# A Fourier filter and mixture-of-experts kernel: first transfers on one queue, a matrix partly built by GpSimd, copies by two engines, stores issued by SP

## The chip, the cores and the metric

The kernel runs on one core of a Trainium2 chip. The metric is the device time of one execution in microseconds. An execution of the kernel before was profiled by the hardware; all rows below are from it.

## What is computed

The reference, cut to what matters:

```python
def _attn_ref(x, filt_r, filt_i):            # x: 8 x 2496 x 256
    X = np.fft.rfft(x, axis=1)
    Y = X * (filt_r + 1j * filt_i)[None]
    return np.fft.irfft(Y, n=x.shape[1], axis=1)

def _moe_ref(x, w_gate, w1, w2):             # 19968 tokens x 256, 8 experts
    logits = x @ w_gate
    order = np.argsort(-logits.flatten())
    for idx in order:                        # each expert takes up to N / E tokens
        ...
    for e in range(E):
        h = np.maximum(x[mask] @ w1[e], 0.0)
        out[mask] = h @ w2[e]
```

Everything is float32.

## The kernel before

The transform along the 2496 positions is split as 39 x 64. For each of the 8 batches there are these steps, all as matrix products on TensorE:

- **s1** (`Fft.s1`, line 201): 43 products of a 117-row slice of x with the constant `cS1`, in 11 tiles `t` of four products (the last has three). Each tile's result in PSUM is copied into `Y1` by four copies (line 207), `cp` and `ri` each 0 and 1. The PSUM pool has two such tiles (tag "a"). Each product stands in the trace as two records.
- **s2** (`Fft.s2`, line 214): ten units (g, dh), each four products of `Y1` with the second-step matrix `cW`; VectorE multiplies the result by the filter `F` (lines 220, 221), GpSimd combines the halves (lines 222, 223).
- **tr, trv** (lines 233, 242, 261): transposes back, and the logits' products with the gate.
- **inv1** (lines 269 to 283): ten inverse units q per batch, with the constants `cEh` and `cEl`; the result is copied to a tile `zt` (`ZB` = 4 buffers) and stored by two DMAs of 64 rows to `zd[b]` in DRAM.

Later `inv2` reads `zd` back and finishes the inverse; then the tokens are routed to experts, gathered, and run through two layers (lines 785 to 886). That later part is most of the span.

`Fft.run` puts steps into time slots with priorities (`at(slot, priority, ...)`), ten slots for a batch, and emits them in that order: s1 of batch b in slots 10b-10 to 10b, s2 from 10b, tr three and inv1 five slots behind. Batch b+1's s1 is so interleaved with batch b's s2. The tile framework's scheduler then orders each engine's queue; each engine runs its queue in order. Every DMA issued by SP or ACT takes the next of eight DMA semaphores, and a DMA that takes one again first waits for the transfer that had it.

The start, before: `consts` builds `cW`, 20 blocks of 128 x 128, each from `ab` and `cs` (one small load): ACT scales (line 154), VectorE multiplies and adds (line 155, two inputs in SBUF). `F` (2.6 MB) is loaded by two DMAs on ACT's queue (line 163); x of batch 0 by ten DMAs on SP's queue (line 189), x of batch 1 behind them; `consts3` stores zeros into the pads of the eight `zd` from ACT's queue (line 175) and loads `cEh` and `cEl` from GpSimd's queue once x of batch 1 is there (lines 178, 179). In batch 0 ACT makes all four copies of an even tile t, VectorE those of an odd one. The inverse units' stores are issued by ACT (line 283).

Of the kernel before, what the change touches and what calls it, by code (L numbers as in the profile page):

```python
# [7 lines left out]
F32, F32R = mybir.dt.float32, mybir.dt.float32r  # L8
# [101 lines left out]
def lay_filter(re, im):  # L110

    k, j = np.arange(K1)[:, None], np.arange(J)[None]
    fr = np.where(j < 32, k + 39 * j, 39 * (j - 31) - k)
    f = np.stack([np.asarray(re)[fr], np.asarray(im)[fr]])
    return np.ascontiguousarray(f.reshape(2, K1, J, 2, 128).transpose(4, 3, 1, 0, 2)).reshape(128, -1)


def lay_w1(w):
# [9 lines left out]
class Fft:  # L128
# [11 lines left out]
    def consts(s):  # L140
        nc, i = s.nc, s.i
        t = lambda n, sh: s.cp.tile(sh, F32, name=n)
        s.cS1 = t("cS1", [117, 120])
        s.F = s.wp.tile([128, 2, K1, 128], F32, name="F", tag="F", bufs=1)
        nc.sync.dma_start(s.cS1, i['cS1'])
        s.cW = s.wp.tile([128, K1, 128], F32, name="cW", tag="cW", bufs=1)
        q = s.wp.tile([128, 4, 128], F32, name="P", bufs=NP).rearrange("p k (m d) -> p (k m d)", m=1)
        nc.scalar.dma_start(q[:, :296], i['cW'])
        w = t("warm", [1, 2])
        nc.vector.memset(w, 0.0)  # L150
        nc.scalar.copy(w[:, 1:], w[:, :1])
        ab, cs = q[:, :256], q[:, 256:]
        for k in range(K1):
            nc.scalar.activation(s.cW[:, k], ab[:, :128], AF.Copy, scale=cs[:, k:k+1])
            nc.vector.scalar_tensor_tensor(s.cW[:, k], ab[:, 128:], cs[:, K1+k:K1+k+1], s.cW[:, k], op0=OP.mult, op1=OP.add)

    def consts2(s):
        nc, i = s.nc, s.i
        t = lambda n, sh, dt=F32: s.cp.tile(sh, dt, name=n)
        s.Vh, s.Vl = (s.cp.tile([128, K1, 64], F32R, name=n, tag=n, bufs=1) for n in ("Vh", "Vl"))  # L160
        s.id, s.gate = t("fid", [128, 128]), t("gate", [128, 2, 32])
        for dh in range(2):
            nc.scalar.dma_start(s.F[:, dh], i['filt'].rearrange("p (h k j) -> p h k j", h=2, k=K1)[:, dh])
        make_identity(nc, s.id)
        nc.gpsimd.memset(s.gate, 0.0)
        for h in range(2):
            nc.sync.dma_start(s.gate[:, h, :8], i['moe_w_gate'][128*h:128*h+128])

    def consts3(s):
        nc, i = s.nc, s.i  # L170

        q = s.wp.tile([128, 4, 128], F32, name="Q", bufs=1)
        nc.gpsimd.memset(q, 0.0)
        for zd in s.zd:
            nc.scalar.dma_start(zd[:, N2:], q[:40].rearrange("p k (n d) -> p (k n d)", n=1).rearrange("p (n d) -> p n d", n=2))
        s.cE = [s.cp.tile([128, K1, 128], F32R, name=n) for n in ("cEh", "cEl")]
        for c, nme in zip(s.cE, ("cEh", "cEl")):
            nc.gpsimd.tensor_copy(c[64:65, 0, :1], s.xr[1, 1][64:65, 0, 0, :1])
            nc.gpsimd.dma_start(c, i[nme].rearrange("p (k q) -> p k q", k=K1))

    def load_x(s, b, h, parts=1):

        w = 24 - 5*h
        xr = s.xr[b, h] = s.xp.tile([117, w, 2, N2], F32, name=f"xr{h}", bufs=2)
        v = s.i['x'][b].rearrange("p (q c n) -> p q c n", c=2, n=N2)
        for k in range(parts):
            q0, q1 = w*k//parts, w*(k+1)//parts
            for r in (slice(0, 112), slice(112, 117)):
                s.nc.sync.dma_start(xr[r, q0:q1], v[r, 24*h+q0:24*h+q1])

    def s1(s, b, t):

        nc = s.nc
        if t == 0:
            s.Y1[b] = s.wp.tile([128, K1, D], F32, name="Y1", tag="Y1", bufs=2)
        h = t // 6
        xv = s.xr[b, h].rearrange("p q c n -> p q (c n)")
        p = s.ps.tile([128, 4, 128], F32, name="p1", tag="a", bufs=2)
        q0, q1 = 4*t, min(4*t+4, 43)
        for q in range(q0, q1):  # L200
            s.lastmm = nc.tensor.matmul(p[:, q-q0, :120], xv[:, q-24*h], s.cS1, start=True, stop=True).ins  # L201
        for cp in range(2):
            for ri in range(2):
                src = p[64*cp:64*cp+64, :q1-q0, :120].rearrange("p q (b r k) -> p r k b q", b=3, r=2)[:, ri]
                a = s.Y1[b][64*ri:64*ri+64, :, 43*cp+q0:43*cp+q0+1]
                dst = bass.AP(tensor=a.tensor, offset=a.offset, ap=[list(a.ap[0]), [a.ap[1][0], K1], [85, 3], [1, q1-q0]])
                (nc.vector.tensor_copy if t in ((5,) if b else (1, 3, 5, 7, 9)) else nc.scalar.copy)(dst, src)  # L207

    def s2(s, b, g, dh):

        nc = s.nc
        p = s.ps.tile([128, 4, 128], F32, name="p2", tag="b", bufs=2)
        for k in range(4):
# [168 lines left out]
    def run(s, cp, wp, xp, ps, freed, prep, rest):  # L382
# [711 lines left out]
```

## Time and profile before

| | us |
|---|---|
| median of 3 runs (lowest, highest) | 1464.4 (1460.85, 1466.78) |
| the profiled execution's own time | 1464.14 |
| its span, first to last instruction | 1461.9 |
| TensorE busy in the span | 1387.9 |
| VectorE / ACT / GpSimd busy | 912.8 / 682.9 / 493.2 |
| first product of s1, batch 0 | 6.06 |
| first product of s2, batch 0 / 1 / 7 | 43.4 / 73.8 / 293.8 |

The own time is the span and 2.2 us around it. Engines in the rows are PE (TensorE matmul), PEld (its weight load), DVE (VectorE), ACT, POOL (GpSimd) and SP; a q behind the name is the engine's queue, which issues DMAs and waits. `out<-in` are tile names, `xN` a count. In a row of the timeline the bracket gives the idle time ahead of the piece and what ended it.

### The profile page before, as it was taken

To read this page: it belongs to the slowest core of one execution; us is meant where nothing else is said; L and a number is where in the kernel's file an instruction comes from. 1 tells how busy PE (TensorE), PEld (TensorE's weight loads), DVE (VectorE), ACT (ScalarE), POOL (GpSimd) and SP (SyncE) were. 2 spreads that over 40 slices of the span, in tenths; PEclk is the share of its full clock that TensorE was granted. 3 is DMA by queue.
4 is the path that set the end of the run, shared out by engine and by line. 5 is a ranking of instruction groups with operands and counts; after the bars stand their busy time and mean duration, and the time that the engine had idled before them with its cause. 6 is when DMAs were issued, how large, how long until landed. Compare 5 with 4: busy or idle time off the path is not lost.

```text
span 1461.9 us, 27147 instructions
## 1 busy us (share of the span) xinstructions
PE 1387.9 (95%) x10310; PEld 1214.2 (83%) x10310; DVE 912.8 (62%) x2589; ACT 682.9 (47%) x1676; POOL 493.2 (34%) x530
## 2 busy tenths in 40 slices
PE   4999999998896999999999999999999999999998
PEld 4998899985543898888889888898888899989988
DVE  3665666753666768767876977967876845333231
ACT  3666666644565425434533633633632635433232
POOL 0343333440102413522632443443325433333212
PEclk9999999998997999999999999999999999999999
DMA  9665564559996102212211211211211321111100
GB/s 266 182 165 141 145 176 99 119 157 280 297 352 219 57 26 91 64 36 75 69 43 58 73 50 48 86 48 41 98 34 54 132 70 46 39 48 49 42 23 27
DMA packets 56248, 150.60 MB, mean 103 GB/s; under 512 B 10824, under 2 KB 31432, under 8 KB 51921
## 3 DMA queue, kind: packets, MB, share of 16 engines
q0 software_dynamic: 17840, 60.34, 12.7%
q10 hardware_dynamic: 29407, 46.10, 10.5%
q1 hardware_dynamic: 8872, 42.44, 10.3%
q8 instruction: 81, 1.33, 0.4%
q14 instruction: 48, 0.39, 0.1%
HBM read 85.17 MB, written 63.70 MB: 102 GB/s over the span
## 4 chain that ended last, share of the span: by engine, by line
PE 68%; DVE 9%; issue 9%; ACT 6%; DMA 4%; ACTq 2%; POOL 2%; POOLq 0%; SPq 0%; DVEq 0%
PE py L867 23%; PE pz L824 22%; PE p L201 4%; PE pv L375 4%; PE p L214 4%; PE pa L269 2%; ACT Y L207 2%; PE rt L538 2%; PE ptr L802 2%; ACTq L283 2%; PE pa L233 2%; POOL out L878 1%; DMA xs<-xo 1%; ACT lg L698 1%; DMA wr<-w,widx 1%
## 5 line engine op out<-in xcount | busy, mean ns | idle before, releaser
L867 PE MATMUL py<-w1h,hl 128*128 128x256 f32 x2496 | 482.6, 286 | 1.1 <-DVE hl L835 1.0
L867 PEld LDWEIGHTS py<-w1h,hl 128*128 128x128 f32 x2496 | 401.1, 191 | 3.9 <-DVE hl L835 1.7
L867 PE MATMUL py<-w1l,hl 128*128 128x256 f32 (+1 forms) x1280 | 359.1, 282 | 0.0
L878 POOL DMA_INDIRECT out<-y,oid x160 | 171.9, 1074 | 495.6 <-ACT y L877 461.2
L830 ACT ACTIVATE hl<-pz 128x512 fp32r<-128x512 f32 (+1 forms) x320 | 187.2, 587 | 229.7 <-PE pz L824 206.1
L824 PE MATMUL pz<-xo,w0h 128*128 128x512 f32 (+1 forms) x640 | 263.9, 412 | 6.5 <-DVE hl L832 4.8
L832 DVE SCALAR_TENSOR_TENSOR hl<-pz,hl 128x512 fp32r<-128x512 f32 x256 | 174.9, 687 | 127.4 <-ACT hl L830 126.5
L824 PE MATMUL pz<-xo,w0l 128*128 128x512 f32 (+1 forms) x640 | 248.5, 388 | 0.0
L824 PE MATMUL pz<-z,w0h 128*128 128x512 f32 (+1 forms) x640 | 248.2, 388 | 0.3 <-DVE z L806 0.3
L867 PEld LDWEIGHTS py<-w1l,hl 128*128 128x128 f32 (+1 forms) x1280 | 241.1, 188 | 1.9
L788 POOL DMA_INDIRECT xg<-xs,xid x160 | 176.4, 1102 | 127.0 <-issue 44.5
L877 ACT COPY y<-py 128x256 f32<-128x256 f32 x152 | 56.4, 372 | 302.2 <-PE py L867 278.9
L207 ACT COPY Y<-p 64x240 f32<-64x240 f32 (+1 forms) x304 | 116.0, 382 | 60.7 <-PE pv L242 15.7
L824 PEld LDWEIGHTS pz<-xo,w0h 128*128 128x128 f32 x640 | 121.6, 190 | 24.8 <-DVE hl L832 6.2
L824 PEld LDWEIGHTS pz<-xo,w0l 128*128 128x128 f32 x640 | 120.6, 188 | 23.7
L824 PEld LDWEIGHTS pz<-z,w0h 128*128 128x128 f32 x640 | 121.7, 190 | 16.2 <-DVE z L806 0.9
L201 PE MATMUL p<-cS,xr 117*128 117x120 f32 x688 | 103.0, 299 | 29.3 <-ACT Y L207 20.1
L201 PEld LDWEIGHTS p<-cS,xr 117*128 117x128 f32 x688 | 93.7, 212 | 33.7 <-ACT Y L207 22.8
L222 POOL TENSOR_TENSOR P<-P 128x256 f32<-128x256 f32 x80 | 58.5, 732 | 172.4 <-DVE P L220 171.3
L530 DVE TENSOR_TENSOR Gm<-M,thr 117x1232 bf16<-117x1232 f32 (+2 forms) x80 | 104.4, 1315 | 0.2
L214 PE MATMUL p<-cW,Y 128*128 128x128 f32 x640 | 89.1, 278 | 0.7 <-ACT Y L207 0.7
L214 PEld LDWEIGHTS p<-cW,Y 128*128 128x128 f32 x640 | 80.2, 193 | 2.3 <-issue 1.0
(216 smaller groups left out, 2008.6 us busy)
## 6 DMA issues: line engine op xcount, KB each, us to landing
zd<-zt ACTq DMA_DIRECT2D x160, 128.0 KB
z<-zd SPq DMA_DIRECT2D x26, 600.0 KB
xs<-xo ACTq DMA_DIRECT2D x22, 600.0 KB
xr<-x SPq DMA_DIRECT2D x7, 1344.0 KB
xr<-x SPq DMA_DIRECT2D x7, 1064.0 KB
xs<-Y ACTq DMA_DIRECT2D x10, 600.0 KB
F<-filt ACTq DMA_DIRECT2D x2, 1280.0 KB
xg<-xs,xid POOLq DMA_INDIRECT x160, 2.8
```

The costliest lines, as they stand in the source:

```text
L201: s.lastmm = nc.tensor.matmul(p[:, q-q0, :120], xv[:, q-24*h], s.cS1, start=True, stop=True).ins
L207: (nc.vector.tensor_copy if t in ((5,) if b else (1, 3, 5, 7, 9)) else nc.scalar.copy)(dst, src)
L214: nc.tensor.matmul(p[:, k], s.Y1[b][:, 4*g+k, dh*128:dh*128+128], s.cW[:, 4*g+k], start=True, stop=True)
L222: nc.gpsimd.tensor_tensor(P[:, :, :64], P[:, :, :64], P[:, :, 64:], op=OP.subtract)
L375: nc.tensor.matmul(p[:120, :w], s.cD, z[:, g-g0:g-g0+w], start=True, stop=True)
L530: nc.vector.tensor_tensor(Gm[:, s0:s1, :m], s.M[:, s0:s1].unsqueeze(2).to_broadcast([117, s1 - s0, m]), thr[:117].unsqueeze(1).to_broadcas ...
L788: s.lastg = s.nc.gpsimd.indirect_dma_start(out=xg[:n], out_offset=None, in_=s.xs, in_offset=bass.IndirectOffsetOnAxis(ap=ids[0][:n, t:t+1] ...
L824: nc.tensor.matmul(p[:, :n], w[:, sl], x[:, k, :n], start=m == 0, stop=m == 5)
L830: s.lasta = nc.scalar.activation(h[:, :n], p[:, :n], AF.Relu).ins
L832: nc.vector.scalar_tensor_tensor(l[:, :n], p[:, :n], 0.0, h[:, :n].bitcast(F32), op0=OP.max, op1=OP.subtract)
L867: nc.tensor.matmul(p[:a.stop-a.start], hs[g][f][:, a], b[:, 256*f:256*f+256], start=m == 0, stop=m == 8 * len(terms) - 1, skip_group_check ...
L878: st = nc.gpsimd.indirect_dma_start(out=out_rows, out_offset=bass.IndirectOffsetOnAxis(ap=ids[1][:w, 4*g+t:4*g+t+1], axis=0), in_=y[:w], i ...
```

## The change

- `F`'s layout becomes five groups of g, each [2, 4, 128] per partition, and is loaded by five DMAs. All first loads go on SP's queue in order of need: x of batch 0 in five parts, then by turns one group of `F` and one part of x of batch 1. The gate's two small loads go to ACT's queue.
- The zero stores go to SP's queue, behind the first load of batch 2, from a tile of their own.
- ACT and VectorE build only blocks 0 to 7 of `cW`. GpSimd builds 8 to 19: for each g of 2, 3, 4 two products of 128 x 512 and one sum.
- `cEh` and `cEl` are loaded in two pieces each (blocks 0 to 7, then 8 to 19), from GpSimd's queue, when the first and the fifth unit of s2 are through.
- In batch 0 ACT makes the copies of `cp` 0 and VectorE those of `cp` 1, for every tile.
- Batches 0 to 5 have their inverse stores issued by SP; 6 and 7 still by ACT.

```diff
@@ consts
-        s.F = s.wp.tile([128, 2, K1, 128], F32, name="F", tag="F", bufs=1)
+        s.F = s.wp.tile([128, 5, 2, 4, 128], F32, name="F", tag="F", bufs=1)
...
-        for k in range(K1):
+        for k in range(8):
             nc.scalar.activation(s.cW[:, k], ab[:, :128], AF.Copy, scale=cs[:, k:k+1])
             nc.vector.scalar_tensor_tensor(s.cW[:, k], ab[:, 128:], cs[:, K1+k:K1+k+1], s.cW[:, k], op0=OP.mult, op1=OP.add)
+        for g in range(2, 5):
+            t = s.wp.tile([128, 2, D], F32, name="zt", bufs=ZB).rearrange("p k (m d) -> p (k m) d", m=2)
+            for m, o in enumerate((s.cW[:, 4*g:4*g+4], t)):
+                nc.gpsimd.tensor_tensor(o, ab[:, 128*m:128*m+128].unsqueeze(1).to_broadcast([128, 4, 128]),
+                                        cs[:, K1*m+4*g:K1*m+4*g+4].unsqueeze(2).to_broadcast([128, 4, 128]), op=OP.mult)
+            nc.gpsimd.tensor_tensor(s.cW[:, 4*g:4*g+4], s.cW[:, 4*g:4*g+4], t, op=OP.add)
@@ consts2
-        for dh in range(2):
-            nc.scalar.dma_start(s.F[:, dh], i['filt'].rearrange("p (h k j) -> p h k j", h=2, k=K1)[:, dh])
+        s.cE = [t(n, [128, K1, 128], F32R) for n in ("cEh", "cEl")]
+        for k, g in zip("FxFxFxFxFx", (0, 0, 1, 1, 2, 2, 3, 3, 4, 4)):
+            if k == "F":
+                nc.sync.dma_start(s.F[:, g], i['filt'][g].rearrange("p (h k j) -> p h k j", h=2, k=4))
+            else:
+                s.load_x(1, g // 3, *((g, 3) if g < 3 else (g - 3, 2)))
...
         for h in range(2):
-            nc.sync.dma_start(s.gate[:, h, :8], i['moe_w_gate'][128*h:128*h+128])
+            nc.scalar.dma_start(s.gate[:, h, :8], i['moe_w_gate'][128*h:128*h+128])
@@ consts3 becomes load_E and zeros
-            nc.scalar.dma_start(zd[:, N2:], q[:40].rearrange("p k (n d) -> p (k n d)", n=1).rearrange("p (n d) -> p n d", n=2))
...
-            nc.gpsimd.tensor_copy(c[64:65, 0, :1], s.xr[1, 1][64:65, 0, 0, :1])
-            nc.gpsimd.dma_start(c, i[nme].rearrange("p (k q) -> p k q", k=K1))
+    def load_E(s, g, k0, k1):
+        for c, nme in zip(s.cE, ("cEh", "cEl")):
+            s.nc.gpsimd.tensor_copy(c[:1, k0, :1], s.yt[0, g, 0][:1, 0, :1])
+            s.nc.gpsimd.dma_start(c[:, k0:k1], s.i[nme].rearrange("p (k q) -> p k q", k=K1)[:, k0:k1])
+    def zeros(s):
+        for zd in s.zd:
+            s.nc.sync.dma_start(zd[:, N2:], s.zero)
@@ s1
-                (nc.vector.tensor_copy if t in ((5,) if b else (1, 3, 5, 7, 9)) else nc.scalar.copy)(dst, src)
+                (nc.vector.tensor_copy if (t == 5 if b else cp) else nc.scalar.copy)(dst, src)
@@ inv1
-            nc.scalar.dma_start(s.zd[b].rearrange("a n c -> n a c")[:N2, 20*r+2*q:20*r+2*q+2], zt[64*r:64*r+64])
+            (nc.scalar if b >= B - 2 else nc.sync).dma_start(s.zd[b].rearrange("a n c -> n a c")[:N2, 20*r+2*q:20*r+2*q+2], zt[64*r:64*r+64])
@@ run
-        at(-12, 0, s.load_x, 0, 0, 3)
-        at(-12, 0, s.load_x, 0, 1, 2)
+        for k in range(5):
+            at(-12, 0, s.load_x, 0, k // 3, *((k, 3) if k < 3 else (k - 3, 2)))
         at(-12, 2, s.consts2)
-        for h in range(2):
-            at(-12, 3, s.load_x, 1, h)
-        at(-12, 4, s.consts3)
+        at(0.5, 1.5, s.load_E, 0, 0, 8)
+        at(4.5, 1.5, s.load_E, 2, 8, K1)
+        at(12, 9, s.zeros)
```

Lines behind the edits move: in the changed kernel s1's copy is line 217, s2's product 224, the inverse store 293.

ACT's queue at the start before, between its first loads and its first copies of s1:

```order
L163 DMA F<-filt 128x2560 x2
L175 DMA zd_60<-Q 40x512
L154 ACTIVATE cW<-P 128x128 x20
L175 DMA zd_61<-Q 40x512
L175 DMA zd_62<-Q 40x512
L175 DMA zd_63<-Q 40x512
L175 DMA zd_64<-Q 40x512
L175 DMA zd_65<-Q 40x512
L175 DMA zd_66<-Q 40x512
L175 DMA zd_67<-Q 40x512
L207 COPY Y_180<-p_181 64x20x3x4 x4
L207 COPY Y_180<-p_199 64x20x3x4 x4
```

and the same place with the change:

```order
L148 DMA P<-cW 128x296
L151 ACT_TABLE_LOAD
L151 COPY warm<-warm 1x1
L178 DMA gate<-moe_w_gate 128x8 x2
L154 ACTIVATE cW<-P 128x128 x8
L217 COPY Y_165<-p_166 64x20x3x4 x2
L217 COPY Y_165<-p_175 64x20x3x4 x2
```

The loads of `F` and all eight zero stores are gone from ACT's queue; ahead of its first copies stand eight scalings and two small loads.

GpSimd's queue with the change, from the identity matrix to the first pieces of `cEh` and `cEl` (P at line 159 is the tile of the small load; before, nothing of line 159 or 161 was there):

```order
masks.py:199 AFFINE_SELECT fid<-fid 128x128
L159 TENSOR_TENSOR cW<-P 128x512
L159 TENSOR_TENSOR zt<-P 128x512
L161 TENSOR_TENSOR cW<-cW,zt 128x512 x3
L232 TENSOR_TENSOR P<-P 128x4x64
L233 TENSOR_TENSOR P<-Q 128x4x64
L183 CAST cEh<-P 1x1
L183 CAST cEl<-P 1x1
L184 DMA cEh<-cEh 128x1024
L232 TENSOR_TENSOR P<-P 128x4x64
L184 DMA cEl<-cEl 128x1024
```

The two rows of line 159 stand there three times; nine instructions of 128 x 512 come ahead of GpSimd's part of s2. VectorE's queue with the change, from its start:

```order
L150 MEMSET warm 1x2
L155 SCALAR_TENSOR_TENSOR cW<-P,cW 128x128 x8
L217 COPY Y_165<-p_166 64x20x3x4 x2
L217 COPY Y_165<-p_175 64x20x3x4 x2
L217 COPY Y_165<-p_184 64x20x3x4 x2
```

All eight of line 155 stand ahead of VectorE's first copy of s1; before, nine stood there, and eleven more between its first three sets of copies.

SP's queue with the change, where batch 0's inverse stores begin (xr_461 and xr_705 are batch 3's x, xr_959 the first part of batch 4's):

```order
L199 DMA xr_461<-x 112x3072
L199 DMA xr_461<-x 5x3072
L293 DMA zd_60<-zt 64x2x256 x4
L199 DMA xr_705<-x 112x2432
L199 DMA xr_705<-x 5x2432
L293 DMA zd_60<-zt 64x2x256 x12
L199 DMA xr_959<-x 112x3072
L199 DMA xr_959<-x 5x3072
L293 DMA zd_60<-zt 64x2x256 x4
L293 DMA zd_61<-zt 64x2x256 x4
```

Before, SP's queue held only the loads of x there; the stores stood in ACT's queue between its copies.

## Rows read from the trace of the kernel before

**Rows 1.** The page's first line.

```profile
span 1461.9 us, 27147 instructions
```

**Rows 2.** By stretch: length, busy of PE, PEld, DVE, ACT, POOL; PEclk, DMA share, GB/s.

```profile
14.00:26.00 12.00, 0.01 (x1) 0.00 (x0) 0.62 (x3) 1.54 (x5) 0.00 (x0) 1.00 0.97 278
26.00:43.40 17.40, 16.42 (x71) 15.42 (x72) 6.50 (x16) 7.46 (x20) 1.63 (x4) 1.00 0.96 289
43.40:73.80 30.40, 30.40 (x280) 28.70 (x280) 20.09 (x35) 21.23 (x56) 14.57 (x20) 1.00 0.54 146
73.80:293.80 220.00, 210.86 (x2120) 198.33 (x2119) 148.52 (x273) 150.02 (x394) 89.55 (x135) 1.00 0.55 142
```

**Rows 3.** Timeline of PE, first 60 us: start, length, engine, line, operation, count.

```profile
6.06 3.74 PE L201 MATMUL p<-cS,xr 117*128 117x120 f32 x16 [6.06 <-DMA xr<-x]
...
26.02 14.99 PE L201 MATMUL p<-cS,xr 117*128 117x120 f32 x62 [12.01 <-ACT Y L207]
41.54 2.03 PE L201 MATMUL p<-cS,xr 117*128 117x120 f32 x8 [0.53 <-PE p L201]
43.37 1.93 PE L214 MATMUL p<-cW,Y 128*128 128x128 f32 x8
...
47.42 1.05 PE L201 MATMUL p<-cS,xr 117*128 117x120 f32 x8
...
57.89 0.37 PE L269 MATMUL pa<-yh,cEh 128*128 128x256 f32 x1
```

**Rows 4.** Timeline of ACT, first 45 us.

```profile
6.76 5.07 ACT L154 ACTIVATE cW<-P 128x128 f32<-128x128 f32 x17 [3.42 <-DMA P<-cW]
...
16.63 7.69 ACTq L175 DMA_DIRECT2D zd<-Q  x6
24.37 3.20 ACT L207 COPY Y<-p 64x240 f32<-64x240 f32 x8 [11.66 <-DMA zd<-Q]
```

**Rows 5.** The chain of waits in order of time, its first two pieces.

```profile
1.92 10.54 DMA F<-filt
12.78 9.81 DMA xr<-x
```

**Rows 6.** Weight loads of s1 (PEld, line 201) from 26 to 41 and 60 to 290.

```profile
L201 PEld LDWEIGHTS p<-cS,xr 117*128 117x128 f32 x62 | 13.5, 330 | 13.5 <-ACT Y L207 12.3 <-PE p L201 1.2
...
L201 PEld LDWEIGHTS p<-cS,xr 117*128 117x128 f32 x542 | 66.1, 192 | 10.8 <-ACT Y L207 10.5
```

**Rows 7.** Timeline of DVE, first 45 us.

```profile
7.20 2.69 DVE L155 SCALAR_TENSOR_TENSOR cW<-P,cW 128x128 f32<-128x128 f32 x9 [6.33 <-DMA xr<-x]
...
28.12 1.66 DVE L207 COPY Y<-p 64x240 f32<-64x240 f32 x4 [13.50 <-PE p L201]
```

**Rows 8.** Timeline of POOL and DVE, 369 to 379; DVE line 548: lowest, median, longest ns.

```profile
375.63 1.93 POOL L255 TENSOR_TENSOR yl<-Y,yh 128x512 fp32r<-128x512 f32 x1 [1.76 <-ACT yh L254]
377.50 1.30 POOL L255 TENSOR_TENSOR yl<-P,yh 128x512 fp32r<-128x512 f32 x1
...
377.72 1.16 DVE L548 TENSOR_TENSOR X<-D,row 112x56 f16<-112x56 f32 x1
...
L548 DVE TENSOR_TENSOR X<-D,row x77: 156/197/1162, 372.0 to 1130.8; 112x56 f16<-112x56 f32 x9, 112x49 f16<-112x49 f32 x9, 112x42 f16<-112x42 f32 x9, 112x35 f16<-112x35 f32 x9
```

**Rows 9.** What PE waited for, 73.8 to 293.8; ACT's timeline near 190.

```profile
PE p L201 <- ACT Y L207: 8.1, 13, 1.4
...
188.03 2.58 ACTq L283 DMA_DIRECT2D zd<-zt  x4
190.66 0.38 ACT L207 COPY Y<-p 64x240 f32<-64x240 f32 x1 [2.07 <-PE pv L242]
```

**Rows 10.** DMA issues: KB each, median us to landing; POOL's timeline at 34.

```profile
cEh<-cEh POOLq DMA_DIRECT2D x1, 1280.0 KB, 9.8
...
34.01 0.75 POOL L179 DMA_DIRECT2D cEh<-cEh  x1 [0.30 <-POOL cEl L178]
```

**Rows 11.** What SP's queue waited for, first 400 us: total, times, longest.

```profile
SPq L189 <- PE p L201: 65.1, 8, 14.0
```

More of the change, by code (lines that the diff above doesn't have):

```diff
@@ L114, in lay_filter @@
     f = np.stack([np.asarray(re)[fr], np.asarray(im)[fr]])
-    return np.ascontiguousarray(f.reshape(2, K1, J, 2, 128).transpose(4, 3, 1, 0, 2)).reshape(128, -1)
+    return np.ascontiguousarray(f.reshape(2, 5, 4, J, 2, 128).transpose(1, 5, 4, 2, 0, 3)).reshape(5, 128, -1)
 def lay_w1(w):
@@ L160, in consts2 @@
         s.Vh, s.Vl = (s.cp.tile([128, K1, 64], F32R, name=n, tag=n, bufs=1) for n in ("Vh", "Vl"))
-        s.id, s.gate = t("fid", [128, 128]), t("gate", [128, 2, 32])
-        for dh in range(2):
-            nc.scalar.dma_start(s.F[:, dh], i['filt'].rearrange("p (h k j) -> p h k j", h=2, k=K1)[:, dh])
+        s.id, s.gate, s.zero = t("fid", [128, 128]), t("gate", [128, 2, 32]), t("zero", [40, 2, D])
+        s.cE = [t(n, [128, K1, 128], F32R) for n in ("cEh", "cEl")]
[4 more added lines that the diff above has]
+                s.load_x(1, g // 3, *((g, 3) if g < 3 else (g - 3, 2)))
@@ L164, in consts2 @@
         make_identity(nc, s.id)
         nc.gpsimd.memset(s.gate, 0.0)
+        nc.gpsimd.memset(s.zero, 0.0)
         for h in range(2):
-            nc.sync.dma_start(s.gate[:, h, :8], i['moe_w_gate'][128*h:128*h+128])
[L169 to L173, printed above, removed]
-        for zd in s.zd:
-            nc.scalar.dma_start(zd[:, N2:], q[:40].rearrange("p k (n d) -> p (k n d)", n=1).rearrange("p (n d) -> p n d", n=2))
-        s.cE = [s.cp.tile([128, K1, 128], F32R, name=n) for n in ("cEh", "cEl")]
-        for c, nme in zip(s.cE, ("cEh", "cEl")):
-            nc.gpsimd.tensor_copy(c[64:65, 0, :1], s.xr[1, 1][64:65, 0, 0, :1])
-            nc.gpsimd.dma_start(c, i[nme].rearrange("p (k q) -> p k q", k=K1))
@@ L181, in load_x @@
-    def load_x(s, b, h, parts=1):
+            nc.scalar.dma_start(s.gate[:, h, :8], i['moe_w_gate'][128*h:128*h+128])
[4 more added lines that the diff above has]
+    def zeros(s):
+        for zd in s.zd:
+            s.nc.sync.dma_start(zd[:, N2:], s.zero)
+    def load_x(s, b, h, k=0, parts=1):
@@ L183, in load_x @@
         w = 24 - 5*h
-        xr = s.xr[b, h] = s.xp.tile([117, w, 2, N2], F32, name=f"xr{h}", bufs=2)
+        if k == 0:
+            s.xr[b, h] = s.xp.tile([117, w, 2, N2], F32, name=f"xr{h}", bufs=2)
+        xr = s.xr[b, h]
         v = s.i['x'][b].rearrange("p (q c n) -> p q c n", c=2, n=N2)
[L186 to L189, printed above, removed]
+        q0, q1 = 4*((w+3)//4*k//parts), min(4*((w+3)//4*(k+1)//parts), w)
@@ L191, in s1 @@
+        for r in (slice(0, 112), slice(112, 117)):
+            s.nc.sync.dma_start(xr[r, q0:q1], v[r, 24*h+q0:24*h+q1])
     def s1(s, b, t):
@@ L216, in s2 @@
         Q = s.wp.tile([128, 4, 128], F32, name="Q", bufs=1)
-        F = s.F[:, dh, 4*g:4*g+4]
+        F = s.F[:, g, dh]
         a = F[:, :, 64:65]
```

## The prediction

> **What bounds the kernel now.** First the sums by stretch [rows 2]. From 73.8 to 293.8 us TensorE is busy 210.86 of 220.00 us, so there TensorE is the limit and at most 220.00 - 210.86 = 9.1 us are to be had. From 14 to 26 us TensorE does nothing, at a DMA share of 0.97. The start is where the time lies. All that comes behind it hangs on TensorE's progress through the eight batches, so what s2 of batch 0 gains at its first product, at 43.37 us [rows 3], moves the rest forward as a whole, if nothing new holds it.
>
> Second, TensorE's timeline [rows 3]. Two tiles of s1 run at 6.06 us (16 records in 3.74 us); at 26.02 us TensorE starts again after 12.01 us in which it waited for ACT's copy of `Y`. Third, ACT's timeline at that place [rows 4]: its queue stands in the zero stores from 16.63 us for 7.69 us, and the first copy starts at 24.37 us, released by such a store. A store there waits for one of the eight DMA semaphores, so behind `F` and x. In the chain of waits [rows 5] this start is two transfers, `F` (10.54 us from 1.92) and x (9.81 us from 12.78). The two queues share the same traffic: x, which TensorE needs at once, came beside `F`, which nobody needs before 45 us.
>
> Fourth, the speed of TensorE. The clock column reads 1.00 throughout the first 74 us [rows 2], but a weight load of s1 takes 330 ns between 26 and 41 us and 192 ns later [rows 6], and eight records take 2.03 us at 41.54 and 1.05 us at 47.42 [rows 3]. So up to about 45 us TensorE was at the lower of its two levels (1.2 and 2.4 GHz), whatever the column says. Before it rose it had worked without a gap since 41.54 us, some 4 us; from 26 us on it had paused after every two tiles, the last time 0.53 us ahead of 41.54 (17.40 - 16.42 = 1.0 us in all [rows 2]).
>
> **The change part by part.** The sum is made against the profiled execution, 1464.1 us (span 1461.9 [rows 1] and 2.2 around it), 0.3 below the median of the runs.
>
> *Loads in order, zeros off ACT, copies by two engines.* These go together. The start of TensorE stays at about 6.1 us, since the first part of x already came ahead of `F`. The small load of `ab` and `cs` stays at 6.8 us, where ACT starts on it [rows 4]. With `F` behind it, x of batch 0 (2.6 MB, at the 278 GB/s of [rows 2] 9.3 us) is in by about 13 us. ACT now has eight scalings of 5.07 / 17 = 0.30 us, then copies. VectorE's eight multiply-adds take 2.69 / 9 x 8 = 2.4 us from 7.2 us on [rows 7], if nothing holds them, so its first copies would begin at 9.6 us. A tile's two copies take each engine 2 x 1.66 / 4 = 0.83 us [rows 7], so TensorE would go on at 9.6 + 0.83 + 0.1 = 10.6 us instead of 26.
>
> *`cW` by GpSimd: where I put the largest cost.* GpSimd's first product and VectorE's first multiply-add start together, when the small load lands. Both read two tiles in SBUF. The trace of before has this meeting once, far from here [rows 8]: a VectorE TENSOR_TENSOR of line 548, 197 ns in the median, took 1.16 us from 377.72, and ended at 378.88, just behind GpSimd's product of two SBUF tiles (377.50 to 378.80). So VectorE stood until GpSimd was nearly through. GpSimd's product of 128 x 512 took 1.30 us; the change has nine of that size, with some 0.08 us between, and eight multiply-adds on VectorE. If one multiply-add gets through per GpSimd instruction, the eighth ends with GpSimd's eighth, at 6.9 + 8 x 1.38 = 17.9 us and some tenths: 18.1. Bounds: no blocking (9.6 us), or one per instruction at the 1.93 us that GpSimd's longest one took while VectorE was in its way (6.9 + 8 x 2.01 = 23). I take one per instruction, 18.1 us, since [rows 8] is the same pair of engines with the same kinds of operands. It is the Trainium skill, "SBUF — State Buffer", section "Who interferes with whom", that makes this a rule: a VectorE instruction with two SBUF inputs and a GpSimd instruction that reads SBUF exclude each other, and the second to start waits for the whole of the first. The row shows it for a TENSOR_TENSOR; no row shows it for line 155's kind. By the rule the sum is the one below, by VectorE's own row [rows 7] without it the first rival's.
>
> *From there to s2.* TensorE resumes at 18.1 + 0.83 + 0.1 = 19.0 us, nine tiles left. At the lower level a tile takes 3.74 / 2 = 1.87 us [rows 3], more than the copies need; so TensorE works without a gap, and after 4 us, as from 41.54 us, I take it to rise. By 23 us 2.1 tiles are done. At the higher level a tile is 0.9 us of products; with copies (0.83) and the hand-overs (about 0.4) over two buffers it is (0.9 + 0.83 + 0.4) / 2 = 1.07 us: 6.9 x 1.07 = 7.4 us, so s1 ends at 30.4, and with the last copies and hand-overs (1.2 us) s2 begins at 31.6. Gain 43.4 - 31.6 = **11.8 us**. Had the level stayed low, nine tiles take 16.8 instead of 11.4 us: gain 6.4.
>
> *The lower level's tail.* The 2 us after 43.4 ran at half speed and won't: **1.0 us**.
>
> *Inverse stores to SP.* ACT's queue spends 2.58 us on four of them at 188.03, and the copy behind waits 2.07 us, marked as if for TensorE [rows 9]; the one large wait of TensorE in the eight batches is for ACT's copies, 8.1 us in 13 waits. Batches 0 to 5 are freed of 120 issues, at 0.65 us 77 us of ACT's queue. What TensorE can gain is between nothing and 9.1 us; VectorE's side of the same pipeline stays. I take two thirds, **6 us**. Against it stands the Trainium skill, "DMA: Bandwidth & Descriptors", section "Issuing engines are not separate DMA queues": choosing the issuing engine saves only its issue time, usually small beside the transfer. By that this part is about nothing and the time 6 us longer; the row at 190.66 speaks against it.
>
> *`cEh`, `cEl` in pieces.* GpSimd's queue now issues four loads inside s2; one took it 0.75 us [rows 10], with the casts about 2 us per pair. VectorE's `Q` has one buffer, so a late GpSimd can hold VectorE and then TensorE: 0 to 3 us, I take **1 us** lost, as GpSimd is busy only 14.57 of 30.40 us there. The first inverse needs the pieces 57.89 - 43.37 = 14.5 us behind s2's begin; a whole `cEh` landed in 9.8 us, and the first two pieces are 1 MB together, issued some 4 us behind s2's begin: about level, covered because `F` and x of batch 1 (5.2 MB, 19 us) are through by 32 us. If that cover went, it is 0 to 3 us.
>
> *The rest costs nothing.* GpSimd's nine instructions end at 6.9 + 9 x 1.38 = 19.3 us, with VectorE's share at 22, before s2 begins. The zero stores (0.6 MB) go behind batch 2's first load; only `inv2` reads them, near the end of the eight batches, and SP's queue had room. The gate's two small loads stand on ACT while it waits for the small load anyway.
>
> Sum: -11.8 - 1.0 - 6 + 1 = -17.8, so 1464.1 - 17.8 = 1446.3, **1446 us**.
>
> **The rivals.**
> *Less blocking than one per instruction.* If two multiply-adds slip through per GpSimd instruction, VectorE is free at about 13.6 us, 4.4 us earlier: 1442. If none is held, it is 9.6 us: 8.5 us earlier, 1437.7. For it: a multiply-add has 128 elements in a row and takes 0.35 us, about the pause between two GpSimd instructions; against it: [rows 8].
> *ACT's relief gives nothing.* TensorE's waits move to VectorE's copies or GpSimd: 1446 + 6 = 1452. For it: DVE is busy 148.52 of 220 us, as much as ACT's 150.02 [rows 2].
> *The level stays low, or GpSimd's products are longer.* The first costs 16.8 - 11.4 = 5.4 us, the second (1.93 us each) 23 - 18.1 = 4.9 us: 1451.
> *Slower: stores stuck behind x on SP.* SP's queue waited 65.1 us in 8 waits for TensorE to release x's buffers, at most 14.0 us [rows 11]; now 12 and 4 and 4 stores by turns stand behind such loads. An inverse unit comes every 220 / 60 = 3.7 us and `zt` has four buffers, so a store may be three units late, 11 us, before a copy waits for its buffer, then ACT or VectorE, then TensorE. At 14.0 us it costs 3 us for each of ten loads: 1446 + 30 = 1476. Against it: the order puts the s1 tile that releases x ahead of the inverse unit whose store stands behind that load, so the wait is over when the store is due.
>
> **How the numbers follow.** About 0.5% (7.3 us) is what a measurement of this kernel can tell from no change. The forecast has 0.45, its own range 1443 to 1450; less blocking 0.32; no relief 0.08; low level or longer products 0.08; stores stuck 0.04; small losses adding up to no change 0.03. Range 1435 to 1453: from 1437.7 less the 3 us of relief that I left out, to 1452 and one more. Faster: 0.45 + 0.32 + 0.08 + 0.08 = 0.93; same 0.03; slower 0.04.
>
> **What would show it.** In the changed kernel's timeline: VectorE's multiply-adds of 128 x 128 spread over 6.9 to 18 us, with GpSimd's products beside them; TensorE's second pair of tiles at about 19 us, s2's first product at 31.6; ACT's first copies straight behind its scalings; weight loads of s1 at 190 ns before s2 begins; the wait of s1 for ACT's copies far below 8.1 us between batch 1 and batch 7. Wrong: multiply-adds back to back in 2.4 us (then s2 near 23 us), s2's first product later than 37 us, TensorE waiting for `cEh`, or copies to `zt` that wait for a store.

## The result and the profile after

The changed kernel takes 1449.5 us (median of 5 runs, 1446.5 to 1452.6), the kernel before 1464.0 (5 runs): a ratio of 0.9897, with a 95% interval of 0.9881 to 0.9913. The forecast was 1446, from 1435 to 1453. The total is right; its split is not, as the rows show. The profiled execution took 1449.9 us.

By stretch, the changed kernel (columns as in [rows 2]):

```profile
0.00:36.00 36.00, 22.92 (x98) 21.44 (x99) 17.56 (x31) 12.61 (x34) 11.31 (x17) 1.00 0.99 240
36.00:66.00 30.00, 29.30 (x279) 27.13 (x277) 19.58 (x34) 22.67 (x59) 17.28 (x28) 1.00 1.04 266
66.00:104.00 38.00, 35.14 (x343) 33.57 (x344) 24.37 (x44) 24.30 (x63) 13.63 (x19) 0.96 0.59 149
104.00:290.00 186.00, 186.00 (x1916) 176.99 (x1916) 136.03 (x249) 133.88 (x342) 82.54 (x126) 1.00 0.57 144
```

and two of these stretches in the kernel before:

```profile
0.00:36.00 36.00, 15.47 (x66) 14.46 (x67) 10.75 (x34) 13.57 (x38) 2.89 (x12) 1.00 0.93 267
...
104.00:290.00 186.00, 176.86 (x1770) 166.01 (x1770) 124.16 (x228) 127.29 (x335) 74.15 (x113) 1.00 0.54 137
```

From 104 to 290 us TensorE now never stops: 1916 matmul records in the time in which it did 1770. Up to 36 us it does 98 where it did 66, but the transfers are slower, 240 GB/s against 267, at a DMA share of 0.99.

The start, in the timelines of DVE, POOL, ACT and PE of the changed kernel (they answer to [rows 7, 8, 4, 3]):

```profile
6.38 8.57 DVE L155 SCALAR_TENSOR_TENSOR cW<-P,cW 128x128 f32<-128x128 f32 x8 [5.52 <-ACT cW L154]
...
18.91 0.84 DVE L217 COPY Y<-p 64x240 f32<-64x240 f32 x2 [2.25 <-ACT Y L217]
```

```profile
6.00 1.03 POOL L159 TENSOR_TENSOR cW<-P 128x512 f32<-128x512 f32 x1 [4.14 <-DMA P<-cW]
7.00 1.08 POOL L159 TENSOR_TENSOR zt<-P 128x512 f32<-128x512 f32 x1
...
12.23 3.84 POOL L161 TENSOR_TENSOR cW<-cW,zt 128x512 f32<-128x512 f32 x3
```

```profile
18.12 0.76 ACT L217 COPY Y<-p 64x240 f32<-64x240 f32 x2 [7.81 <-PE p L211]
```

```profile
16.05 3.74 PE L211 MATMUL p<-cS,xr 117*128 117x120 f32 x16 [6.53 <-DMA xr<-x]
...
33.39 2.03 PE L211 MATMUL p<-cS,xr 117*128 117x120 f32 x8 [0.15 <-PE p L211]
35.22 1.46 PE L224 MATMUL p<-cW,Y 128*128 128x128 f32 x8
...
68.86 0.39 PE L279 MATMUL pa<-yh,cEl 128*128 128x256 f32 x1 [3.48 <-DMA cEl<-cEl]
...
70.86 1.92 PE L224 MATMUL p<-cW,Y 128*128 128x128 f32 x8
...
75.87 1.06 PE L224 MATMUL p<-cW,Y 128*128 128x128 f32 x8
```

Eight multiply-adds take 8.57 us beside GpSimd's first eight instructions: six products, one every 1.04 us, and two of the three sums, one every 1.27 us. They end at 14.95 us, the eighth GpSimd instruction at 14.80. At 16.05 us TensorE resumes, behind VectorE's first copies (from 14.96 us); the row names x, but `e2_pool_late`, below, resumes at the same tile at 10.94 us. VectorE's copies of a tile (18.91) begin when ScalarE's of the same tile (18.12, 0.76 us) are through. s2 begins at 35.22 us, 8.2 earlier than at [rows 3]. At 68.86 us TensorE has waited 3.48 us for the second piece of `cEl`, and behind that wait it is at its lower level: eight records take 1.92 us at 70.86 and 1.06 us at 75.87. In the chain of waits the piece is one long step:

```profile
52.34 16.48 DMA cEl<-cEl
```

To compare kernels whose order differs a little, I read from each trace when TensorE begins the matmul record with n others ahead of it: n = 94 is about s2's first, 700 lies near the end of batch 1, 2600 some 10 us behind the begin of batch 7's s2, 3290 where the routing's positions begin. The experiments ran on three chips, where the kernel before took 1490 us (`e1` to `e4`), 1496 us (`e5` to `e8`) and 1464 us (`e9` to `e12`), so times are compared as ratios to the kernel before on the same chip. Among the experiments only the second chip has a ratio of the changed kernel itself (`e5_after_again`). Times in the first four expectations are in the first result's us.

| kernel | n = 94 | 700 | 2600 | 3290 | ratio to before (95%) |
|---|---|---|---|---|---|
| before, first profile | 43.4 | 105.7 | 303.3 | 432.0 | |
| before, `e12_before_again` | 40.2 | 101.0 | 300.1 | 429.7 | |
| changed, first profile | 35.2 | 102.0 | 286.3 | 417.5 | 0.9897 (0.9881 to 0.9913) |
| changed, `e5_after_again` | 33.0 | 100.7 | 285.0 | 416.3 | 0.9855 (0.9831 to 0.9878) |
| `e1_act_stores` | 35.9 | 105.4 | 297.1 | 425.8 | 0.9951 (0.9930 to 0.9973) |
| `e7_before_sp` | 39.2 | 101.5 | 287.1 | 415.7 | 0.9917 (0.9885 to 0.9949) |
| `e2_pool_late` | 26.3 | 97.7 | 282.0 | 413.7 | 0.9839 (0.9815 to 0.9864) |
| `e4_nodep` | 27.9 | 97.6 | 281.9 | 413.6 | 0.9873 (0.9848 to 0.9897) |
| `e3_e_early` | 34.8 | 96.9 | 284.2 | 418.2 | 0.9885 (0.9857 to 0.9913) |
| `e6_all` | 22.3 | 99.8 | 284.0 | 413.2 | 0.9869 (0.9846 to 0.9893) |
| `e8_all_zero` | 21.4 | 92.5 | 278.2 | 411.9 | 0.9862 (0.9840 to 0.9885) |
| `e9_no_gpsimd` | 32.9 | 106.9 | 292.5 | 426.6 | 0.9924 (0.9894 to 0.9954) |
| `e11_f_act` | 36.0 | 97.6 | 283.2 | 411.9 | 0.9931 (0.9907 to 0.9954) |
| `e10_extra` | 34.4 | 101.2 | 285.5 | 421.0 | 0.9927 (0.9901 to 0.9953) |

With the two profiles of each kernel averaged, the change gains 7.7 us at n = 94, 2.0 at 700, 16.0 at 2600 and 14.0 at 3290. So of the start 5.7 us are lost again up to the end of batch 1 (the wait for `cEl` and the lower level behind it are there); 14 us come from 700 to 2600; 2 us go back behind.

### The profile page after: what moved, and what is told of

Its sections match the earlier page's. It is cut to its first block, busy times and chain, and to the rows that moved or that the text cites. A ratio compares the mean times of both kernels' runs of the same rounds, so it can differ in the third digit from the quotient of the medians.

```text
span 1448.1 us, 27257 instructions
## 1 busy us (share of the span) xinstructions
PE 1386.1 (96%) x10310; PEld 1214.4 (84%) x10310; DVE 918.3 (63%) x2579; ACT 683.4 (47%) x1662; POOL 503.9 (35%) x543
## 4 chain that ended last, share of the span: by engine, by line
PE 72%; DVE 9%; issue 8%; DMA 5%; ACT 3%; POOL 2%; ACTq 1%; POOLq 0%; DVEq 0%; SPq 0%
PE py L877 23%; PE pz L834 22%; PE p L211 5%; PE p L224 5%; PE pa L279 4%; PE pv L385 3%; PE pa L243 2%; PE rt L548 2%; PE ptr L812 2%; POOL out L888 1%; PE pv L252 1%; DMA xs<-xo 1%; DMA xr<-x 1%; DMA cEl<-cEl 1%; ACT lg L708 1%
## 5 line engine op out<-in xcount | busy, mean ns | idle before, releaser
L211 PEld LDWEIGHTS p<-cS,xr 117*128 117x128 f32 x688 | 93.6, 212 | 14.6 <-issue 14.6
L540 DVE TENSOR_TENSOR Gm<-M,thr 117x1232 bf16<-117x1232 f32 (+2 forms) x80 | 105.4, 1328 | 0.2
L224 PE MATMUL p<-cW,Y 128*128 128x128 f32 x640 | 92.4, 279 | 0.0
```

Of the source, the lines that this page charges most:

```text
L540: nc.vector.tensor_tensor(Gm[:, s0:s1, :m], s.M[:, s0:s1].unsqueeze(2).to_broadcast([117, s1 - s0, m]), thr[:117].unsqueeze(1).to_broadcas ...
```

## The experiments

**Theory:** ScalarE's relief brings the middle stretch, and the start is held by three things, the blocked multiply-adds, copies that go one after the other, and late transfers. **Rival:** the better start brings it all, and the stores' place is worth nothing.

**The stores' place, from both sides.** In `e1_act_stores` the changed kernel's stores go back to ScalarE; in `e7_before_sp` the kernel before gets them on SP, and nothing else.

```diff
-            (nc.scalar if b >= B - 2 else nc.sync).dma_start(s.zd[b] ...
+            nc.scalar.dma_start(s.zd[b] ...
```

> The changed kernel with the inverse stores issued by ScalarE again, all else kept. Theory (the stores' issues on ScalarE were what held TensorE up in batches 2 to 6): the stretch from the first second-step matmul of batch 2 to that of batch 7, 171.7 us in the changed kernel and 186.2 us before it, comes back to 184 to 187 us, TensorE waits for ScalarE's copies there again, and the kernel takes 1455 to 1464 us, of which the start's gain stays (first second-step matmul at about 35 us). Rival (the shorter stretch comes from the start's better order of transfers and the stores are worth nothing): the stretch stays at 171 to 174 us and the kernel takes 1449 to 1452 us.

> The kernel before with one part of the change alone: the inverse stores of batches 0 to 5 issued by SP, all else as before. Theory (the stores' issues on ScalarE held TensorE up in batches 2 to 6, and this part needs none of the others): the stretch from the first second-step matmul of batch 2 to that of batch 7 falls from 186.2 us to 171 to 174 us, the first second-step matmul stays at about 43 us, and the ratio to the kernel before is 0.990 to 0.994. Rival (SP then holds the stores behind x, or the relief needs the better start): the stretch stays at 180 us or more and the ratio is 0.996 to 1.002.

What TensorE waited for from 104 to 290 us, in `e1_act_stores`:

```profile
PE p L211 <- ACT Y L217: 5.7, 10, 1.2
```

in `e12_before_again`:

```profile
PE p L201 <- ACT Y L207: 8.2, 14, 1.9
```

and by stretch, in `e7_before_sp`:

```profile
104.00:290.00 186.00, 184.22 (x1900) 174.88 (x1900) 133.41 (x246) 134.07 (x344) 80.95 (x122) 1.00 0.58 147
```

From n = 700 to 2600 the two profiles of before take 197.6 and 199.1 us, `e7_before_sp` 185.6, the changed kernel 184.3 both times, `e1_act_stores` 191.7. So the stores' place alone brings 12 to 13.5 us of the 14 and needs none of the other parts; the rival falls. By the expectation's measure, s2 of batch 2 to s2 of batch 7, `e7_before_sp` takes 173.5 us, as expected. Undone, the stores' place costs 7.4 us from 700 to 2600, not 13 (182.7 us by the expectation's measure, a little under its 184 to 187), and 3 to 5 us more ahead of n = 700, which `e1_act_stores` reaches at 105.4 us, no earlier than before (105.7 and 101.0). At n = 2600 the part is worth 14.6 us alone and 11.4 us undone; all other parts together bring 1.5 us there with the stores on SP and 4.7 us with them on ScalarE. How the waits share out between them I can't assign. In the times `e1_act_stores` is 0.5% faster than before, `e7_before_sp` 0.8%; of the latter's six runs three took 1477 us and three 1485 to 1490, so its interval is wide. Still, on the same chip the changed kernel is faster than it (0.9855, and the intervals do not meet): in the times the stores' place alone is 14 of 21 us, though at the positions the two are level (415.7 and 416.3). What makes the rest of the difference stays open.

**The multiply-adds.** Before each GpSimd product one element of its output is written from column 7, which VectorE makes last, so that the products begin behind the multiply-adds:

```diff
             for m, o in enumerate((s.cW[:, 4*g:4*g+4], t)):
+                nc.gpsimd.tensor_copy(o[:1, 0, :1], s.cW[:1, 7, :1])
```

> The changed kernel with GpSimd's products made to start after VectorE's eighth multiply-add (each product's output is first written by a one-element copy out of matrix column 7). Theory (each of VectorE's multiply-adds was held for one GpSimd product): the eight multiply-adds take 0.2 to 0.4 us each and end at about 9 us instead of 14.95, TensorE resumes stage 1 of batch 0 at about 10 us instead of 16.05, the first second-step matmul comes at 29 to 31 us instead of 35.2, and the kernel takes 1443 to 1446 us. Rival (the parts of x or GpSimd's later products bound the start anyway): the multiply-adds end early but TensorE waits for x or for the matrix, the first second-step matmul comes at 33 us or later, and the kernel takes 1448 to 1451 us.

DVE's timeline in `e2_pool_late`,

```profile
7.02 2.40 DVE L155 SCALAR_TENSOR_TENSOR cW<-P,cW 128x128 f32<-128x128 f32 x8 [6.16 <-ACT cW L154]
```

and PE's:

```profile
10.94 3.74 PE L212 MATMUL p<-cS,xr 117*128 117x120 f32 x16 [1.07 <-ACT Y L218]
14.85 1.12 PE L212 MATMUL p<-cS,xr 117*128 117x120 f32 x8 [0.17 <-PE p L212]
```

Eight multiply-adds in 2.40 us instead of 8.57: GpSimd's products did hold them. TensorE resumes at 10.94 us, 5.1 and 5.8 us earlier than in the two profiles of the changed kernel. s2 begins at 26.3, earlier than the 29 to 31 expected, since here TensorE is at its higher level from 14.85 us on, and that differs from execution to execution (below). The ratio, 0.9839, is the lowest of all, but its interval meets that of the changed kernel in `e5_after_again`. `e9_no_gpsimd` takes GpSimd's part away (`for k in range(K1)` in place of `range(8)`, the loop over GpSimd's groups gone):

> The changed kernel without GpSimd's part in the second-step matrix: all 20 columns built by ScalarE and VectorE, as before the change, all else kept (the copies of batch 0 still split between two engines, after the 20 multiply-adds). Theory (GpSimd's products only held VectorE up: with them 8 multiply-adds took 8.57 us, and when they were kept off, the first second-step matmul came at 26.3 us instead of 35.2): 20 multiply-adds without them take 0.2 to 0.35 us each, 4 to 7 us, TensorE resumes stage 1 at 11 to 14 us, the first second-step matmul is at 27 to 33 us, and the time is within 5 us of the changed kernel's. Rival (the part pays as a relief of the two engines): the first second-step matmul comes at 36 us or later and the kernel is slower than the changed one.

Its timeline of DVE:

```profile
7.18 5.90 DVE L155 SCALAR_TENSOR_TENSOR cW<-P,cW 128x128 f32<-128x128 f32 x20 [6.31 <-ACT cW L154]
```

All twenty in 5.90 us; TensorE resumes at 14.60 us (11 to 14 expected) and s2 begins at 32.9, no later than in the changed kernel: as placed, GpSimd's help cost the start as much as it took off. But n = 700 comes 5.6 us later, since TensorE then waits 3.4 us for `cEh` and 6.8 us for `cEl`. In this profile the transfers ran at 236 GB/s in the first 36 us, and the granted clock was 0.77 from 36 to 66 us. The part of the expectation on s2 was met. Whether that on the time was can't be said: 0.9924 is 4 us longer than the changed kernel by its first ratio (0.9897, where the kernel before took the same 1464 us as here) and 10 us by its second.

**Copies side by side.** VectorE's copies of a tile read other partitions of the PSUM tile than ScalarE's and write other columns of `Y1`; the program orders them all the same. `e4_nodep` declares VectorE's independent of ScalarE's in batch 0:

```diff
+                o = (nc.vector.tensor_copy if (t == 5 if b else cp) else nc.scalar.copy)(dst, src)
+                if b == 0:
+                    if cp:
+                        for x in s.cp0:
+                            s.tc.declare_no_dep(o.ins, x.ins, reason="disjoint columns")
...
```

> The changed kernel with VectorE's copies of a tile in stage 1 of batch 0 freed from waiting for ScalarE's copies of the same tile (they read and write other partitions). Theory (the two engines copy one after the other, 1.95 us a tile, and the gap of 0.17 us that this leaves in TensorE's work every two tiles keeps its clock low): the copies run side by side, TensorE works without gaps from about 16 us on, its clock rises in stage 1, and the first second-step matmul comes at 28 to 31 us instead of 35.2; the kernel takes 1443 to 1446 us. Rival (the clock stays low whatever the gaps, or the tiles are bound by TensorE itself): the first second-step matmul comes at 33 to 35 us and the kernel takes 1447 to 1450 us.

The timelines of PE, ACT and DVE in `e4_nodep`:

```profile
16.12 10.51 PE L211 MATMUL p<-cS,xr 117*128 117x120 f32 x62 [0.31 <-DVE Y L217]
```

```profile
18.19 0.78 ACT L217 COPY Y<-p 64x240 f32<-64x240 f32 x2 [1.58 <-PE p L211]
```

```profile
18.19 0.84 DVE L217 COPY Y<-p 64x240 f32<-64x240 f32 x2 [1.35 <-PE p L211]
```

The copies do run side by side; 62 records, 31 products, follow without a stop, and s2 begins at 27.9 us, 5 to 7 us earlier. Not all of this is the copies': VectorE's queue has another order here, two copies ahead of its last two multiply-adds, so that TensorE resumes at 13.77 us. And what I made of the gaps of 0.17 us does not follow. PE's timeline in `e5_after_again`, the very kernel of the first profile, with the same gaps:

```profile
16.69 3.74 PE L211 MATMUL p<-cS,xr 117*128 117x120 f32 x16 [6.82 <-issue]
20.59 3.74 PE L211 MATMUL p<-cS,xr 117*128 117x120 f32 x16 [0.17 <-PE p L211]
24.50 1.12 PE L211 MATMUL p<-cS,xr 117*128 117x120 f32 x8 [0.17 <-PE p L211]
```

Eight records take 1.12 us from 24.50 on, so here TensorE was at its higher level 7.8 us after it resumed; in the first profile eight still took 2.03 us at 33.39, 17 us after it resumed. So the level rose with the same gaps in one execution and not in the other: the theory of the gaps is not shown, and what sets the moment of the rise stays open. `e1`, `e3` and `e10` run the same instructions up to s2 as well; in the five executions s2 began at 33.0, 34.4, 34.8, 35.2 and 35.9 us.

**What the start is worth later.** `e3_e_early` asks for the second pieces of `cEh` and `cEl` at group 1 (`at(2.5, 1.5, s.load_E, 1, 8, K1)` in place of `at(4.5, 1.5, s.load_E, 2, 8, K1)`); `e6_all` joins this with `e2` and `e4`; `e8_all_zero` also lets the zero stores wait for batch 1 (their slot goes from 12 to 15.5):

```diff
     def zeros(s):
+        a = s.yt[1, 2, 0][:1, 0, :1]
+        s.nc.gpsimd.tensor_tensor(s.zero[:1, 0, :1], a, a, op=OP.subtract)
```

> The changed kernel with the second pieces of the two inverse matrices asked for earlier: gated by the first product of group 1 instead of group 2. Theory (the wait of 3.5 us for the second piece at 69 us, with the lower clock that follows it, is a loss of its own): TensorE has no wait for that matrix, no low clock near 70 us, the stretch from the first second-step matmul of batch 1 to that of batch 2 falls from 39.1 to 33 to 35 us, and the kernel takes 1444 to 1447 us. Rival (the piece then collides with the x transfers of batch 1 and 2, or a later wait takes its place): the stretch stays at 37 to 40 us and the kernel takes 1448 to 1451 us.

> The changed kernel with three of the earlier edits together: GpSimd's products after VectorE's multiply-adds, the second pieces of the inverse matrices asked for a group earlier, and VectorE's copies of batch 0 free of ScalarE's. Alone the first and the third brought the first second-step matmul to 26 to 28 us from 35.2, but the first matmul of batch 2's second step only to 98.7 us from 103.0, whichever of them it was. Theory (up to about 65 us the DMA engines are full, share about 1.0, so that a faster start ends in a wait for transfers): the three together come to 96 to 98.5 us at batch 2 although their first second-step matmul is at 22 to 27 us, and the ratio to the kernel before is 0.982 to 0.985. Rival (the three gains add up, 7 + 7 + 3 us): batch 2 at 86 to 92 us and a ratio of 0.976 to 0.980.

> The kernel with the three edits together and one more: the eight stores of zeros, 80 KB each, which SP issues at 30 to 48 us in the changed kernel ahead of x of batch 2, wait for a product of batch 1's group 2 (one element of the zeros is computed from it). Theory (the DMA engines are full up to about 65 us, so 640 KB less in that stretch bring batch 2 forward by their time at the 250 GB/s of the profile, 2.5 us): the first second-step matmul of batch 2 comes 2 to 3 us earlier than with the three edits alone, and the kernel is 1 to 3 us faster than that. Rival (x and the inverse matrices are held by SP's or GpSimd's issues and not by the engines): no difference above 1 us at batch 2.

What TensorE waited for from 26 to 106 us, in `e6_all`:

```profile
PE p L212 <- DMA xr<-x: 6.9, 2, 6.2
PE pa L286 <- DVE zt L298: 5.2, 1, 5.2
```

In `e3_e_early` the wait for `cEl` shrinks from 3.5 to 0.5 us, s2 of batch 1 to s2 of batch 2 takes 35.4 us instead of 39.2 and 40.5 (33 to 35 expected), and the kernel is 4 to 5 us earlier at n = 700; nothing is left of it at 3290. In `e6_all` s2 begins at 22.3 us, 11 to 13 earlier, and at n = 700 the kernel stands 1 to 2 us ahead: TensorE waits 6.9 us for x of batch 1, and 5.2 us for a copy to `zt`. So the three gains do not add up; batch 2's s2 comes at 100.8 us, later than even the theory had it (96 to 98.5), and the ratio is not as good either (0.9869 against 0.982 to 0.985). In `e8_all_zero`, with the 0.64 MB of zeros out of the way, batch 2's s2 comes 5.6 us earlier than in `e6_all` (2 to 3 expected) and n = 700 7.3 us, three times what the bytes explain. The longest wait for x stays at 6.2 us; the wait for `zt` is gone (SP's first inverse stores go out at 50 us instead of 60, no longer behind the zeros). That points to the order of SP's queue beside the bytes; at 3290 the gain is 1.3 us. None of it is seen in the times: 0.9869 and 0.9862 against 0.9855 for the changed kernel on that chip.

**The order on one queue.** `e11_f_act` gives the filter back to ScalarE's queue:

```diff
-                nc.sync.dma_start(s.F[:, g], i['filt'][g] ...
+                nc.scalar.dma_start(s.F[:, g], i['filt'][g] ...
```

> The changed kernel with the five pieces of the filter issued by ScalarE again instead of on SP's queue between the pieces of x, all else kept. Theory (the queue in order of need lets x of batch 0 land first): the filter's 2.6 MB share the engines with x of batch 0, whose last piece lands later; TensorE waits for x in stage 1 of batch 0, the first second-step matmul comes 1 to 5 us later than 33 to 35 us, and the time is 0 to 4 us longer than the changed kernel's. Rival (stage 1 of batch 0 is held by the copies and x is there anyway): the first second-step matmul stays at 33 to 35.5 us, with no difference in time.

By stretch, in `e11_f_act`:

```profile
0.00:36.00 36.00, 22.15 (x95) 20.66 (x95) 17.57 (x31) 12.10 (x32) 11.31 (x17) 1.00 0.94 256
```

s2 begins at 36.0, in the expected range, but the mechanism is not there: TensorE waits for no x once it has begun, and 36.0 is no later than `e1_act_stores` had it (35.9) with the changed kernel's loads. So the order on one queue is not shown to gain anything at s2. n = 700 comes 3 to 4 us earlier: 256 GB/s in the first 36 us instead of 240, and 0.9 us of waiting for `cEl` instead of 3.5. The time (0.9931) does not show that gain: its profiled run, 1444.9 us, is the shortest of nine, up to 1460.

**The stage behind.** `e10_extra` adds a copy of 2.1 MB inside DRAM near 310 us:

```diff
+        s.nc.gpsimd.dma_start(s.dum[0, :1, :1], s.yt[B-1, 4, 0][:1, 0, :1])
+        s.nc.gpsimd.dma_start(s.dum, s.i['filt'][:4])
...
```

> The changed kernel with one needless transfer added: GpSimd's queue copies 2.1 MB of the filter inside DRAM, to a place that nothing reads, once batch 7's last group is multiplied (about 310 us). Theory (from about 300 to 420 us the transfers bound the kernel, share 0.83 to 0.94, 58.2 to 85.6 MB from 330 to 420 us, 304 GB/s, so what is gained at the start is lost there): the extra bytes take 2.1 MB / 304 GB/s = 7 us, and the first matmul of the positions in the routing, at 416 us in the changed kernel, comes 4 to 8 us later. Rival (the stage is bound by TensorE and by single landings, the engines have room): it comes less than 2 us later.

By stretch, from 290 us to the positions, the changed kernel

```profile
290.00:416.90 126.90, 114.29 (x658) 70.49 (x658) 66.42 (x180) 59.66 (x125) 16.07 (x17) 0.95 0.88 278
```

and `e10_extra`

```profile
290.00:420.50 130.50, 115.90 (x654) 71.72 (x652) 64.72 (x179) 59.10 (x125) 16.62 (x19) 0.92 0.88 286
```

From n = 2600 to 3290 it takes 135.5 us, the changed kernel 131.2 and 131.3: 4.2 of the 7 us that 2.1 MB take at 304 GB/s. That points to transfers that bind this stage in part, but one profile does not show it: `e3`, `e8` and `e9` take 133.8 to 134.1 us there without an extra byte. Before, the same stretch took 128.7 and 129.6, in `e7_before_sp` and `e11_f_act` 128.5 and 128.7. So the 2 us that the change gives back here lie within what versions differ by, and their cause stays open.

**The yardsticks.**

> The changed kernel itself, on the chip of the experiments, as their yardstick: earlier its ratio to the kernel before was 0.9897 (0.9881 to 0.9913). Expected under every theory: a ratio of 0.988 to 0.992, first second-step matmul at about 35 us, that of batch 2 at about 103 us, that of batch 7 at about 275 us.

> The kernel before, profiled on the chip of the experiments, for its landmarks there. Expected: the first second-step matmul at 39 to 44 us (43.4 in the first profile; 39.2 in the kernel that differs from it only by the stores), that of batch 7 at 290 to 295 us, the routing's positions at 429 to 433 us, and what follows some 25 us longer than in the first profile, as in the other kernels on this chip.

The changed kernel's ratio came out a little lower than expected, 0.9855; its landmarks agree. Those of before agree too, with s2 at 40.2 instead of 43.4, but `e12_before_again` ran on a chip as fast as the first, so that what follows the positions (some 25 us longer on the slower chips) was not seen for the kernel before there; whether the 0.4% between the two ratios comes from it stays open.

## Why the prediction was right, and where not

**Multiply-adds held by GpSimd: right, mis-sized.** One gets through per GpSimd instruction: eight take 8.57 us beside the products, the eighth ending 0.15 us behind GpSimd's eighth, and 2.40 us when the products begin behind them. The Trainium skill, "SBUF — State Buffer", section "Who interferes with whom", has it that a VectorE instruction with two SBUF inputs contends with a GpSimd instruction that reads SBUF, and that the shared ports are an exclusive lock; the traces agree. The term of 1.38 us, from a subtraction of two tiles on line 255 (1.30) and a pause, came near the sums (1.27) but not the products (1.04), and GpSimd began at 6.00 us instead of 6.9. So VectorE was free at 14.95 us, not 18.1, and TensorE resumed at 16.05, not 19.0. (In the first rival, two per instruction would by the same sum be through at 6.9 + 4 x 1.38 = 12.4 us, not 13.6.)

**From there to s2: two steps wrong.** 0.83 us for "a tile's two copies" took it that the engines work side by side; they take turns, until `e4_nodep` frees them. "After 4 us, as from 41.54 us, I take it to rise" made a rule of one stretch; in two executions of one kernel the level rose 7.8 us and over 17 us after TensorE resumed. The two errors and the shorter products leave s2 at 35.2 and 33.0 instead of 31.6. The gain there is 7.7 us, not 11.8; part of the 43.4 was that one execution's, since the same kernel had s2 at 40.2 in another.

**"Moves the rest forward as a whole, if nothing new holds it": the step that failed most.** The 11.8 and the 1.0 of the tail became 2.0 at n = 700. The transfers are full (a share of 1.04 from 36 to 66 us), and in the faster starts tried here TensorE only arrives earlier at `cEl`, x or `zt`. In the first profile 3.5 of the lost us are the wait for `cEl`; behind it the granted clock is 0.90 from 72 to 80 us, and in `e5_after_again` 0.92 from 66 to 104. No term stood for that lower level. I had called the cover for `cEh` and `cEl` "about level" and priced it at 0 to 3 us; I had not set the bytes up to 66 us against their rate.

**Stores to SP: right in kind, half its size.** I took 6 us, of at most 9.1; it is 12 to 13.5. The bound was false: TensorE's busy time of [rows 2] is no floor. From 104 to 290 us it went from 176.86 to 186.00 us busy, the 9.1 us, and its matmul records from 1770 to 1916, which at 97 ns each is 14.2 us; 5 us of delay lay within what counted as busy. The same shows from n = 700 to 2600: before, 197.6 us with 9.1 idle, so 188.5 busy; in the changed kernel 184.3 us, none idle. The Trainium skill, "DMA: Bandwidth & Descriptors", section "Issuing engines are not separate DMA queues", has it that issuing from several engines saves only the time that the issuing takes, usually small beside the transfer. Here that time stood on the engine whose copies TensorE waits for, and taking it away was worth 12 us and more (`e7_before_sp`).

**Stores stuck behind x: not here, but near.** In the changed kernel two of ScalarE's copies to `zt` wait for a store from 50 to 300 us, 1.1 us together, and TensorE for neither, although SP issues twelve stores over 21 us from 63.45 us on:

```profile
ACT zt L291 <- DMA zd<-zt: 1.1, 2, 0.6
```

In three of the versions with a faster start TensorE itself waits for such a copy: 2.9 us in `e2_pool_late`, 3.7 in `e4_nodep`, 5.2 in `e6_all`; in `e8_all_zero` it does not.

The sum was right by luck: two errors offset each other, 9.8 us too much at the start (11.8 + 1.0 - 1 forecast, 2.0 found), 8 too little from 700 to 2600, and 2 us lost behind: 17.8 - 9.8 + 8 - 2 = 14.0 at the positions, 14.5 in the times. No version here is shown to be faster than the changed kernel; those that stand 3 to 5 us ahead at the positions (`e2`, `e4`, `e6`, `e8`, `e11`) can't be told from it by runs that scatter by 6 us.

## To carry to other kernels

Take the issuing of stores off the engine whose copies the tensor engine waits for, first and alone: here it was one line, the whole gain at the positions and two thirds of it in the times. Before an earlier start is counted, set the bytes that are due up to the next landmark against the rate: here the faster starts ended in waits for transfers. And compare traces by the n-th instruction of the bounding engine, not by a stage's first, since order and busy time both misled here.

## What the hardware showed that I had not expected

- TensorE's level in the first 40 us differs from execution to execution of one kernel: s2 began at 33.0 to 35.9 us in five executions with the same instructions up to there, at 39.2, 40.2 and 43.4 in three of the start before. One profile does not price such a start to better than 3 us.
- One queue with pieces in order of need moved 240 GB/s in the first 36 us, with the filter on a second queue 256, the kernel before 267 and 271, all at a DMA share of 0.92 to 0.99. The size of the pieces differs too; what makes the difference was not tried.
